# Attention and bilinear FFN on one core: weight sums rescheduled, casts halved, one more plain weight pair, result stores merged and moved ahead of transposing loads

## The chip, the cores and the metric

The kernel runs on 1 core of one Trainium2 chip. The metric is the device time of one launch in microseconds (us), lower is better. A few names: TensorE (PE) does the matmuls, VectorE (DVE) and ScalarE (ACT) the elementwise work, GpSimd (POOL) the casts. The SP queue issues almost all DMA transfers, in program order; the transfers themselves run on the core's 16 DMA engines.

## The reference, cut to what matters

```python
# q, k, v: 8 batches x 8 heads x 576 tokens x 64; attention only inside chunks of 64 tokens
scores = scale * q_c @ k_c.T
attn = exp(scores - max) / sum
x = (attn @ v_c) as 4608 tokens x 512
# then the bilinear FFN, w_a and w_b 512 x 1536, w_out 1536 x 512
out = ((x @ w_a) * (x @ w_b)) @ w_out        # 4608 x 512, float32
```

## The kernel before

The 4608 tokens are 9 blocks of 512, each of two units of 256. Attention prepares the units ahead of the FFN blocks. Units 0 to 5 are transposed on TensorE, the others by transposing loads on the SP queue. In block 0, and for the first `PLAIN` weight pairs of block 1, the two products of the FFN are formed plainly. Everywhere else a Strassen-like scheme (`Group`) uses 28 matmuls instead of 32, and needs sums of weights (`combine_w`) and of tokens (`combine_x`), which VectorE forms.

```python
def combine_w(i):                       # four sums, all at once
    ...
    for o, x0, x1, op in ((t1, b12, b11, SUB), (t3, b22, b12, SUB),
                          (t2, t3, b11, ADD), (t4, b21, t2, SUB)):
        nc.vector.tensor_tensor(out=o, in0=x0, in1=x1, op=op)

def bring(U):                           # a later unit: cast, transposing loads, next loads
    cast(U, "qk"); load(U + 1, "q")
    transpose_dma(U)                    # on the SP queue
    cast(U, "v"); load(U + 1, "kv")

def out_part(K, tg, part):              # a third of one 128-token result tile
    ...
    if part == 2:
        o_sb = o_pool.tile([128, DM], FP32, name="o_sb")        # 3 buffers
        nc.vector.tensor_copy(out=o_sb, in_=out_ps.pop((K, tg)))
        for g in range(2):              # two stores of 64 consecutive rows
            r0 = K * BLK + 256 * u + 128 * g + 64 * c
            nc.sync.dma_start(out=out[r0:r0 + 64, :], in_=o_sb[g * 64:g * 64 + 64, :])

# block 0
for ft in range(NFT):
    ab_step(0, ft)
    if ft % 2:
        combine_w(ft // 2)
    ...
bring(6); bring(7)                      # before block 1 begins (cut: a loop in the source)
```

One result tile holds two chunks of 64 tokens that lie 128 rows apart in `out`. That is why there are two stores per tile.

The softmax here doesn't subtract the row's maximum and nothing guards it: scores larger than these inputs give would overflow.

Of the kernel before, what the change touches and what calls it, by code (L numbers as in the profile page):

```python
# [8 lines left out]


PE_UNITS = 6
PLAIN = 2


@with_exitstack
def kernel(
# [10 lines left out]
    nc = tc.nc  # L27
# [15 lines left out]
    BLK = 512  # L43
# [13 lines left out]
    x_pool = ctx.enter_context(tc.tile_pool(name="xp", bufs=3))  # L57
    s_pool = ctx.enter_context(tc.tile_pool(name="sp", bufs=2))
    ab_pool = ctx.enter_context(tc.tile_pool(name="ab", bufs=2))
    b_pool = ctx.enter_context(tc.tile_pool(name="bsb", bufs=2))  # L60
    c_pool = ctx.enter_context(tc.tile_pool(name="csb", bufs=2))
    o_pool = ctx.enter_context(tc.tile_pool(name="osb", bufs=3))
    psum = ctx.enter_context(tc.tile_pool(name="psum", bufs=4, space=PSUM))
# [14 lines left out]
    def bank(pool=None):  # L78
        if pool is None:
            pool = spread[0]  # L80
            spread.append(spread.pop(0))
        n = {id(psum): "ps", id(psum_b): "pb", id(psum_c): "pc"}[id(pool)]
        return pool.tile([128, 512], FP32, name=n)
# [20 lines left out]
    def cast_ab(i):  # L104
        for n in ("wb", "wa"):
            w_ab[n, i] = wpool.tile([128, NKT, WCOL], FP16, name=f"{n}{i}")
            nc.gpsimd.tensor_copy(out=w_ab[n, i], in_=staged.pop((n, i)))

    w_t = {}

    def combine_w(i):
        wb, wa = w_ab["wb", i], w_ab["wa", i]
        b11, b12, b21, b22 = wb[:, 0:2], wa[:, 0:2], wb[:, 2:4], wa[:, 2:4]
        t1, t2, t3, t4 = [
            wpool.tile([128, 2, WCOL], FP16, name=f"t{j}_{i}") for j in range(1, 5)
        ]
        for o, x0, x1, op in (
            (t1, b12, b11, SUB),
            (t3, b22, b12, SUB),
            (t2, t3, b11, ADD),  # L120
            (t4, b21, t2, SUB),
        ):
            nc.vector.tensor_tensor(out=o, in0=x0, in1=x1, op=op)
        w_t[i] = (t1, t2, t3, t4)

    def load_wo(i):
        staged["wo", i] = st_pool.tile([128, 2, DM], FP32, name="st")
# [4 lines left out]

    def cast_wo(i):
        t = wpool.tile([128, 2, DM], BF16, name=f"wo{i}")
        nc.gpsimd.tensor_copy(out=t, in_=staged.pop(("wo", i)))
        for f in range(2):
            w_out[2 * i + f] = t[:, f, :]


# [48 lines left out]
    def transpose_pe(U, names="qk"):  # L188
        if U not in qkt:
            qkt[U] = qkt_pool.tile([128, 2, 2, NKT, 128], BF16, name="qkt")  # L190
        for n in names:
            w = "qk".index(n)
            src = raw.pop((n, U))
            tp = bank().bitcast(BF16).rearrange("c (i m p) -> c i m p", i=2, m=NKT)
            for i in range(2):
                for m in range(NKT):
                    nc.tensor.transpose(
                        tp[:, i, m, :],
                        src[:, i, 2 * m:2 * m + 2, :].rearrange("p j d -> p (j d)"),
                        identity,  # L200
                    )
            dst = qkt[U][:, w].rearrange("c g m (p i) -> c i m g p", i=2)
            for i in range(2):
                cp = nc.vector.tensor_copy if w == 0 or U == 1 else nc.scalar.copy
                cp(out=dst[:, i], in_=tp[:, i].rearrange("c m (g p) -> c m g p", g=2))
# [98 lines left out]
    def bring(U):  # L304

        cast(U, "qk")
        load(U + 1, "q")
        if U < NU:
            transpose_dma(U)
        cast(U, "v")  # L310
        load(U + 1, "kv")
# [9 lines left out]
    def ab_step(K, ft, c0=0, c1=BLK):  # L321
        xT = x_tiles[K]
        dst = ab_tile(K)
        i, o = divmod(ft * 128, WCOL)
        ps = {}
        for n, pool in (("wb", psum_b), ("wa", psum_c)):
            ps[n] = bank(pool if c1 - c0 == BLK else psum)[:, :c1 - c0]
            for kt in range(NKT):
                nc.tensor.matmul(
                    ps[n],  # L330
                    w_ab[n, i][:, kt, o:o + 128],
                    xT[:, kt, c0:c1],
                    start=(kt == 0),
                    stop=(kt == NKT - 1),
                )
        b_sb = b_pool.tile([128, BLK], FP32, name="b_sb")
        nc.scalar.copy(out=b_sb[:, :c1 - c0], in_=ps["wb"])
        nc.vector.tensor_tensor(
            out=dst[:, ft, c0:c1], in0=ps["wa"], in1=b_sb[:, :c1 - c0], op=MULT
        )  # L340
# [17 lines left out]
    class Group:  # L358
# [22 lines left out]
                        skip_group_check=True,  # L381
                    )

        def staged(self, src, name, pool):
            t = pool.tile([128, 512], FP32, name=name)
            nc.scalar.copy(out=t, in_=src)  # L386
            return t

# [5 lines left out]

        def p6(self):
            self.product(self.B, self.t2, self.s2)
            self.u = self.staged(self.B, "u_sb", c_pool)

        def p2(self):
            self.product(self.A, self.b21, self.x12)  # L400
            self.b = self.staged(self.A, "b_sb", b_pool)

        def p5(self):
            self.product(self.B, self.t1, self.s1)
            self.v = self.staged(self.B, "v_sb", c_pool)

        def p7(self):
            self.C = bank(psum_c)
# [25 lines left out]
    def out_part(K, tg, part):  # L434
        if part == 0:
            out_ps[K, tg] = bank(psum)
        for ft in range(4 * part, 4 * part + 4):
            nc.tensor.matmul(  # L438
                out_ps[K, tg],
                ab_tiles[K][:, ft, tg * 128:tg * 128 + 128],  # L440
                w_out[ft],
                start=(ft == 0),
                stop=(ft == NFT - 1),
            )
        if part == 2:
            u, c = divmod(tg, 2)
            o_sb = o_pool.tile([128, DM], FP32, name="o_sb")
            nc.vector.tensor_copy(out=o_sb, in_=out_ps.pop((K, tg)))  # L448
            for g in range(2):
                r0 = K * BLK + 256 * u + 128 * g + 64 * c  # L450
                nc.sync.dma_start(out=out[r0:r0 + 64, :], in_=o_sb[g * 64:g * 64 + 64, :])

    def out_step(K, tg, parts=1):
        u, c = divmod(tg, 2)
# [23 lines left out]
    with tc.manual_schedule(  # L478
# [51 lines left out]
        load(4)  # L530
        load(5)
        spread[:] = [psum]
        for ft in range(NFT):
            ab_step(0, ft)
            if ft % 2:
                combine_w(ft // 2)
            if ft == 6:
                transpose_pe(2)
            if ft == 7:
                slot(2)  # L540
            if ft == 9:
                slot(None, 2)
# [1 line left out]
        cast(4)  # L544
        cast(5)
        load(6)
        for U in range(PE_UNITS, 8):
            bring(U)

        outs = []  # L550

        def chunk():
            if outs:
                out_part(*outs.pop(0))

        def values_x(U):
            values(U)
            if U % 2:
                combine_x(U // 2)

        for ft in range(2 * PLAIN):
            ab_step(1, ft, 0, 256)
            if ft == 0:
                transpose_pe(3)
            if ft == 2:
                scores(3)
        sums(3)
        inverse(3)
        values_x(3)
        for ft in range(2 * PLAIN):  # L570
            ab_step(1, ft, 256, 512)

        attention = {
            (1, PLAIN, 0): [lambda: transpose_pe(4)],
            (1, PLAIN, 1): [lambda: scores(4)],
            (1, PLAIN + 1, 0): [lambda: sums(4), lambda: inverse(4), lambda: transpose_pe(5)],
            (1, PLAIN + 1, 1): [lambda: scores(5)],
            (1, PLAIN + 2, 0): [lambda: values_x(4)],
            (1, PLAIN + 2, 1): [lambda: sums(5)],
            (1, PLAIN + 3, 0): [lambda: inverse(5)],  # L580
            (1, PLAIN + 3, 1): [lambda: values_x(5), lambda: scores(6)],
            (2, 0, 0): [lambda: sums(6), lambda: inverse(6)],
            (2, 0, 1): [lambda: values_x(6)],
            (2, 1, 0): [lambda: scores(7)],
# [28 lines left out]
        for K in range(1, NBLK):  # L613
            for i in range(PLAIN if K == 1 else 0, NWP):
                if (K, i) in ((1, PLAIN), ) or (K > 1 and i == 1):
                    outs += [(K - 1, tg, p) for tg in range(4) for p in range(3)]
                if K > 1 and i in (0, 3):
                    if K == 2 and i == 0:
                        bring(8)
                    if K + 1 < NBLK:  # L620
                        bring(2 * K + 5 if i == 0 else 2 * K + 6)
                now = Group(K, i)
                now.p1()
                if last:
                    last.add7()
                chunk()
                if last:
                    last.p3()
                attend(K, i, 0)
                now.p6()  # L630
                now.p2()
                if last:
                    last.p4()
                chunk()
                if K == 1:
                    chunk()
                attend(K, i, 1)
                now.p5()
                now.p7()
                last = now  # L640
# [39 lines left out]
```

## Time and profile before

The first measurement gave a median of 331.14 us (3 runs, 330.89 to 333.21).

| what | value | view |
|---|---|---|
| TensorE busy | 303.6 of 330.1 us | the page, part 1 |
| 103 to 320 us: TensorE busy | 216.37 of 217 us, clock 1.00 | windows |
| 18 to 47 us: VectorE busy | 23.91 of 29 us | windows |
| mean of one weight sum (24 of them) | 0.77 us | groups: (5.5 + 4.8 + 4.2 + 4.0) / 24 |
| result stores | 70, 2.4 us to landing | DMA issues |

The table of windows follows: busy time of each engine with instruction counts, then the granted TensorE clock, the mean busy share of the 16 DMA engines (it can pass 1) and GB/s.

```profile
18.00:47.00 29.00, 25.00 (x180) 11.45 (x179) 23.91 (x36) 11.34 (x19) 19.42 (x18) 0.94 1.07 316
94.50:103.00 8.50, 7.96 (x112) 5.29 (x110) 6.04 (x11) 4.95 (x9) 1.04 (x1) 0.81 0.88 197
103.00:320.00 217.00, 216.37 (x2216) 152.11 (x2214) 148.22 (x241) 121.16 (x218) 27.05 (x26) 1.00 0.56 117
```

From 103 us on, TensorE has no idle time to give back. Everything that can be gained lies earlier. Two of TensorE's longer waits in the timeline follow (start, duration, instruction, in brackets the idle time and who ended it). One of 2.80 us for `xT`, from 55.8 us, lies between them and is left out here:

```profile
36.25 0.64 PE L228 MATMUL ps<-qkt 64*64 64x64 bf16 x32 [2.11 <-DVE qkt L205]
...
92.23 0.63 PE L228 MATMUL ps<-qkt 64*64 64x64 bf16 x30 [3.33 <-DVE o_sb L448]
```

The second wait leads to the SP queue. Its timeline shows the first result stores at 87.66 us, behind loads and transposing loads (L210). The `o_sb` of the first store was ready at 68.3 us.

```profile
82.99 1.25 SPq L210 DMA_TRANSPOSE qkt<-k_raw  x1
84.28 1.23 SPq L156 DMA_DIRECT2D st<-in_k_dram  x2
85.55 2.01 SPq L156 DMA_DIRECT2D st<-in_v_dram  x2
87.66 5.64 SPq L451 DMA_DIRECT2D out_dram<-o_sb  x8
```

Later in the same timeline, two q loads behind four stores are issued in 1.32 us together (1.32 to 2.43 us in other such places).

```profile
135.78 6.82 SPq L451 DMA_DIRECT2D out_dram<-o_sb  x4
142.64 1.32 SPq L156 DMA_DIRECT2D st<-in_q_dram  x2
144.08 1.91 SPq L210 DMA_TRANSPOSE qkt<-q_raw  x1
```

### The profile page before, as it was taken

The page shows a single profiled execution, that of the slowest core. Times are in us where ns is not written, and L with a number is a line of the kernel's source. Part 1 is how long each engine was busy: PE and PEld are TensorE (multiplying, and loading weights), DVE is VectorE, ACT ScalarE, POOL GpSimd, SP SyncE. Part 2 cuts the span into 40 slices and gives each one's busy share as a digit, 9 for nine tenths or more (in the row PEclk, how much of TensorE's full clock was granted, in tenths as well). Part 3 has the DMA queues.
Part 4 walks back from the last instruction along what each step waited for, and adds up shares of the span by engine and source line. Part 5 has one row for each costly group of instructions (what it writes and reads, how often), then busy time and mean ns, then how long its engine had stood idle before and what let it go on. Part 6 is the DMA issues. An engine that isn't in the chain of part 4 may idle for free.

```text
span 330.1 us, 7886 instructions
## 1 busy us (share of the span) xinstructions
PE 303.6 (92%) x3222; PEld 205.7 (62%) x3222; DVE 216.7 (66%) x350; ACT 172.2 (52%) x307; POOL 74.6 (23%) x76
## 2 busy tenths in 40 slices
PE   2979784899789999999999999999999999999995
PEld 1534353766556667676777666777776677777743
DVE  3459895746365678587758766857595768666551
ACT  1733355375457655656566566565656464444400
POOL 1566665633213322222121212120000000000000
PEclk9999799999959999999999999999999999999999
DMA  8999999999989999876978596964111111111223
GB/s 238 328 374 284 274 367 230 258 218 246 224 186 236 219 168 233 201 159 162 145 178 179 141 158 163 187 155 110 32 30 38 32 34 34 32 35 43 52 65 96
DMA packets 139331, 53.98 MB, mean 164 GB/s; under 512 B 114592, under 2 KB 133280, under 8 KB 139296
## 3 DMA queue, kind: packets, MB, share of 16 engines
q1 hardware_dynamic: 139136, 53.36, 69.6%
q8 instruction: 25, 0.41, 0.5%
q10 hardware_dynamic: 160, 0.13, 0.2%
q14 instruction: 10, 0.08, 0.1%
HBM read 37.75 MB, written 9.44 MB: 143 GB/s over the span
## 4 chain that ended last, share of the span: by engine, by line
PE 65%; DMA 17%; SPq 8%; DVE 5%; POOL 2%; issue 1%; ACT 1%; ACTq 0%; POOLq 0%; DVEq 0%
PE ps L438 21%; PE pb L375 17%; PE pc L375 11%; PE ps L375 10%; DMA st<-in_moe_w_a_dram 7%; DMA st<-in_q_dram 5%; SPq L156 5%; DMA st<-in_v_dram 4%; PE ps L460 3%; PE ps L243 1%; DVE s L355 1%; SPq L168 1%; SPq L210 1%; PE ps L228 1%; PE ps L276 1%
## 5 line engine op out<-in xcount | busy, mean ns | idle before, releaser
L438 PE MATMUL ps<-wo,ab_sb 128*128 128x512 bf16 x384 | 97.9, 379 | 0.0
L375 PEld LDWEIGHTS <-t 128*128 128x128 f16 x736 | 69.2, 98 | 18.2 <-issue 4.8
L413 DVE TENSOR_TENSOR c_sb<-pc,v_sb 128x512 f32<-128x512 f32 x46 | 31.8, 691 | 55.2 <-ACT v_sb L386 55.2
L375 PE MATMUL pb<-s,t 128*128 128x256 f16 x368 | 56.4, 277 | 0.5 <-ACT u_sb L386 0.5
L375 PE MATMUL ps<-xT,wb 128*128 128x256 f16 x368 | 55.7, 274 | 0.0
L386 ACT COPY u_sb<-pb 128x512 f32<-128x512 f32 x46 | 27.0, 586 | 52.1 <-PE pb L375 52.1
L438 PEld LDWEIGHTS <-ab_sb 128*128 128x128 bf16 x384 | 37.6, 98 | 25.7
L425 DVE TENSOR_TENSOR ab_sb<-pc,c_sb 128x512 bf16<-128x512 f32 x46 | 31.7, 689 | 12.2 <-PE pc L375 11.7
L375 PEld LDWEIGHTS <-wb 128*128 128x128 f16 x368 | 36.3, 99 | 4.5
L425 DVE TENSOR_TENSOR ab_sb<-pb,b_sb 128x512 bf16<-128x512 f32 x46 | 31.5, 685 | 4.4 <-PE pb L375 4.4
L386 ACT COPY v_sb<-pb 128x512 f32<-128x512 f32 x46 | 27.1, 589 | 13.1 <-PE pb L375 12.2
L183 POOL CAST q_raw<-st 128x1024 bf16<-128x1024 f32 x17 | 17.7, 1040 | 71.2 <-DMA st<-in_q_dram 65.6
L414 DVE TENSOR_TENSOR pc<-pc,u_sb 128x512 f32<-128x512 f32 x46 | 31.7, 690 | 0.0
L393 ACT COPY pb<-ps 128x512 f32<-128x512 f32 x46 | 27.3, 594 | 7.7 <-PE ps L375 7.7
L236 ACT ACTIVATE E<-ps 128x512 bf16<-128x512 f32 x34 | 18.6, 594 | 21.8 <-PE ps L228 21.8
L375 PE MATMUL pc<-xT,t 128*128 128x256 f16 x184 | 27.6, 272 | 0.6 <-DVE pc L414 0.5
L375 PE MATMUL pb<-s,wa 128*128 128x256 f16 x184 | 28.1, 276 | 0.0
L375 PE MATMUL pc<-s,t 128*128 128x256 f16 x184 | 28.1, 276 | 0.0
L448 DVE COPY o_sb<-ps 128x512 f32<-128x512 f32 x32 | 21.9, 685 | 9.1 <-PE ps L438 5.0
L183 POOL CAST k_raw<-st 128x1024 bf16<-128x1024 f32 x17 | 17.7, 1040 | 43.8 <-DMA st<-in_k_dram 42.9
L386 ACT COPY b_sb<-ps 128x512 f32<-128x512 f32 x46 | 27.3, 594 | 0.0
L253 ACT ACTIVATE ln<-ps 128x512 f32<-128x512 f32 x34 | 18.6, 595 | 15.6 <-PE ps L243 15.6
(67 smaller groups left out, 312.8 us busy)
## 6 DMA issues: line engine op xcount, KB each, us to landing
out_dram<-o_sb SPq DMA_DIRECT2D x70, 128.0 KB, 2.4
st<-in_v_dram SPq DMA_DIRECT2D x32, 256.0 KB, 4.2
st<-in_q_dram SPq DMA_DIRECT2D x23, 256.0 KB, 4.3
st<-in_k_dram SPq DMA_DIRECT2D x23, 256.0 KB, 3.6
st<-in_moe_w_b_dram SPq DMA_DIRECT2D x6, 512.0 KB, 7.0
st<-in_moe_w_a_dram SPq DMA_DIRECT2D x6, 512.0 KB, 8.0
st<-in_moe_w_out_dram SPq DMA_DIRECT2D x6, 512.0 KB, 7.1
st<-in_q_dram SPq DMA_DIRECT2D x4, 512.0 KB, 5.4
```

Of the source, the lines that this page charges most:

```text
L156: nc.sync.dma_start(out=st[p:p + n, g], in_=src[b, :, s:s + n, :].rearrange("h p d -> p h d"))
L183: eng.tensor_copy(out=raw[n, U], in_=staged.pop((n, U)))
L236: nc.scalar.activation(out=E_of[U][:, j], in_=sc[j], func=AF.Exp, scale=scale)
L253: nc.scalar.activation(out=ln_of[U][:, cl].rearrange("p m n -> p (m n)"), in_=sm[cl], func=AF.Ln)
L375: nc.tensor.matmul(t[:, h * 256:h * 256 + 256], w[:, kt, h * 128:h * 128 + 128], x[:, kt], start=start and h == 0 and kt == 0, stop=h == 1 ...
L386: nc.scalar.copy(out=t, in_=src)
L393: nc.scalar.copy(out=self.B, in_=self.A)
L413: nc.vector.tensor_tensor(out=self.c, in0=self.C, in1=self.v, op=ADD)
L414: nc.vector.tensor_tensor(out=self.C, in0=self.C, in1=self.u, op=ADD)
L425: nc.vector.tensor_tensor(out=self.dst[:, :, c0:c0 + 256], in0=t.rearrange("p (h n) -> p h n", h=2), in1=o.rearrange("p (h n) -> p h n", h=2),
L438: nc.tensor.matmul(out_ps[K, tg], ab_tiles[K][:, ft, tg * 128:tg * 128 + 128], w_out[ft], start=(ft == 0), stop=(ft == NFT - 1),)
L448: nc.vector.tensor_copy(out=o_sb, in_=out_ps.pop((K, tg)))
```

## The change

The intent is to relieve VectorE in block 0 (fewer weight sums there), to shorten its collisions with GpSimd casts (half-size casts), to let more steps be in flight (more buffers), and to get the first stores out earlier and with fewer issues.

```diff
-PLAIN = 2
+PLAIN = 3
 def cast_ab(i):                                   # cast_wo likewise
-            nc.gpsimd.tensor_copy(out=w_ab[n, i], in_=staged.pop((n, i)))
+            for h in (slice(0, 2), slice(2, 4)):
+                nc.gpsimd.tensor_copy(out=w_ab[n, i][:, h], in_=src[:, h])
-    def combine_w(i):
+    def combine_w(i, part):                       # two of the four sums at a time
 ab_step: more PSUM pools for wa, b_sb rotates over four names of c_pool (b_pool dropped)
 out_part:
-            for g in range(2):
-                r0 = K * BLK + 256 * u + 128 * g + 64 * c
-                nc.sync.dma_start(out=out[r0:r0 + 64, :], in_=o_sb[g * 64:g * 64 + 64, :])
+            r0 = K * BLK + 256 * u
+            nc.sync.dma_start(
+                out=out[r0:r0 + 256, :].rearrange("(g c r) d -> c g r d", g=2, c=2)[c],
+                in_=o_sb,
+            )
 block 0:
-            if ft % 2:
-                combine_w(ft // 2)
+            if ft >= 2 * PLAIN + 1:
+                combine_w(*combos.pop(0))         # pairs 3 to 5 (the last two sums in mid block 1), 0 to 2 in block 1's groups
-        for U in range(PE_UNITS, 8):
-            bring(U)
+        bring(6)
+        # bring(7) now inside block 1, in its last group
+        transpose_pe(3)                           # before block 1's steps
 ... (attention of units 3 to 6 shifted accordingly)
```

More of the change, by code (lines that the diff above doesn't have):

```diff
@@ L59 @@
     ab_pool = ctx.enter_context(tc.tile_pool(name="ab", bufs=2))
-    b_pool = ctx.enter_context(tc.tile_pool(name="bsb", bufs=2))
     c_pool = ctx.enter_context(tc.tile_pool(name="csb", bufs=2))
@@ L106, in cast_ab @@
             w_ab[n, i] = wpool.tile([128, NKT, WCOL], FP16, name=f"{n}{i}")
-            nc.gpsimd.tensor_copy(out=w_ab[n, i], in_=staged.pop((n, i)))
+            src = staged.pop((n, i))
+            for h in (slice(0, 2), slice(2, 4)):
+                nc.gpsimd.tensor_copy(out=w_ab[n, i][:, h], in_=src[:, h])
     w_t = {}
-    def combine_w(i):
+    def combine_w(i, part):
         wb, wa = w_ab["wb", i], w_ab["wa", i]
         b11, b12, b21, b22 = wb[:, 0:2], wa[:, 0:2], wb[:, 2:4], wa[:, 2:4]
-        t1, t2, t3, t4 = [
-            wpool.tile([128, 2, WCOL], FP16, name=f"t{j}_{i}") for j in range(1, 5)
-        ]
+        if i not in w_t:
+            w_t[i] = [wpool.tile([128, 2, WCOL], FP16, name=f"t{j}_{i}") for j in range(1, 5)]
+        t1, t2, t3, t4 = w_t[i]
         for o, x0, x1, op in (
-            (t1, b12, b11, SUB),
-            (t3, b22, b12, SUB),
-            (t2, t3, b11, ADD),
-            (t4, b21, t2, SUB),
-        ):
+            ((t1, b12, b11, SUB), (t3, b22, b12, SUB)),
+            ((t2, t3, b11, ADD), (t4, b21, t2, SUB)),
+        )[part]:
             nc.vector.tensor_tensor(out=o, in0=x0, in1=x1, op=op)
-        w_t[i] = (t1, t2, t3, t4)
     def load_wo(i):
@@ L134, in cast_wo @@
         t = wpool.tile([128, 2, DM], BF16, name=f"wo{i}")
-        nc.gpsimd.tensor_copy(out=t, in_=staged.pop(("wo", i)))
+        src = staged.pop(("wo", i))
         for f in range(2):
+            nc.gpsimd.tensor_copy(out=t[:, f], in_=src[:, f])
             w_out[2 * i + f] = t[:, f, :]
@@ L325, in ab_step @@
         ps = {}
-        for n, pool in (("wb", psum_b), ("wa", psum_c)):
-            ps[n] = bank(pool if c1 - c0 == BLK else psum)[:, :c1 - c0]
+        whole = c1 - c0 == BLK
+        for n, pool in (
+            ("wb", psum_b if whole else psum),
+            ("wa", (psum_c, psum)[ft % 2] if whole else psum_c),
+        ):
+            ps[n] = bank(pool)[:, :c1 - c0]
             for kt in range(NKT):
@@ L335, in ab_step @@
                 )
-        b_sb = b_pool.tile([128, BLK], FP32, name="b_sb")
+        b_sb = c_pool.tile([128, BLK], FP32, name=("b_sb", "u_sb", "v_sb", "c_sb")[ft % 4])
         nc.scalar.copy(out=b_sb[:, :c1 - c0], in_=ps["wb"])
@@ L382, in product, with staged @@
                     )
-        def staged(self, src, name, pool):
-            t = pool.tile([128, 512], FP32, name=name)
+        def staged(self, src, name):
+            t = c_pool.tile([128, 512], FP32, name=name)
             nc.scalar.copy(out=t, in_=src)
@@ L396, in p6 @@
             self.product(self.B, self.t2, self.s2)
-            self.u = self.staged(self.B, "u_sb", c_pool)
+            self.u = self.staged(self.B, "u_sb")
         def p2(self):
             self.product(self.A, self.b21, self.x12)
-            self.b = self.staged(self.A, "b_sb", b_pool)
+            self.b = self.staged(self.A, "b_sb")
         def p5(self):
             self.product(self.B, self.t1, self.s1)
-            self.v = self.staged(self.B, "v_sb", c_pool)
+            self.v = self.staged(self.B, "v_sb")
         def p7(self):
@@ L532 @@
         spread[:] = [psum]
+        combos = [(i, p) for i in range(PLAIN, NWP) for p in range(2)]
         for ft in range(NFT):
             ab_step(0, ft)
-            if ft % 2:
-                combine_w(ft // 2)
+            if ft >= 2 * PLAIN + 1:
+                combine_w(*combos.pop(0))
             if ft == 6:
@@ L563 @@
             if ft == 0:
-                transpose_pe(3)
-            if ft == 2:
                 scores(3)
-        sums(3)
-        inverse(3)
-        values_x(3)
+            if ft == 3:
+                sums(3)
+                inverse(3)
+        values(3)
+        while combos:
+            combine_w(*combos.pop(0))
+        combine_x(1)
         for ft in range(2 * PLAIN):
             ab_step(1, ft, 256, 512)
+        combos = [(i, p) for i in range(PLAIN) for p in range(2)]
         attention = {
             (1, PLAIN, 0): [lambda: transpose_pe(4)],
-            (1, PLAIN, 1): [lambda: scores(4)],
-            (1, PLAIN + 1, 0): [lambda: sums(4), lambda: inverse(4), lambda: transpose_pe(5)],
-            (1, PLAIN + 1, 1): [lambda: scores(5)],
-            (1, PLAIN + 2, 0): [lambda: values_x(4)],
-            (1, PLAIN + 2, 1): [lambda: sums(5)],
-            (1, PLAIN + 3, 0): [lambda: inverse(5)],
-            (1, PLAIN + 3, 1): [lambda: values_x(5), lambda: scores(6)],
+            (1, PLAIN, 1): [lambda: scores(4), lambda: transpose_pe(5)],
+            (1, PLAIN + 1, 0): [lambda: sums(4), lambda: inverse(4)],
+            (1, PLAIN + 1, 1): [lambda: values_x(4), lambda: scores(5)],
+            (1, PLAIN + 2, 0): [lambda: sums(5), lambda: inverse(5), lambda: bring(7)],
+            (1, PLAIN + 2, 1): [lambda: values_x(5), lambda: scores(6)],
             (2, 0, 0): [lambda: sums(6), lambda: inverse(6)],
@@ L626 @@
                 chunk()
+                if K == 1:
+                    chunk()
+                    combine_w(*combos.pop(0))
                 if last:
@@ L636 @@
                     chunk()
+                    combine_w(*combos.pop(0))
                 attend(K, i, 1)
```

## The prediction

> **What bounds the kernel now.** The table of windows gives TensorE 216.4 busy of 217.0 us between 103 and 320 us at clock 1.00: that part is TensorE-bound and not touched. Before 18 us the first loads set the pace. The losses lie between 18 and 103 us (TensorE busy 71.0 of 85, partly at half clock). The timeline shows them:
>
> - 34.1 us: 2.1 us idle; scores of unit 2 wait for VectorE's copy of the transposes. Half clock follows (1.5 us lost).
> - 47.0 and 49.4 us: 1.0 and 2.05 us; block 1 waits for VectorE (xT, ab_sb).
> - 55.8 us: 2.8 us; second half of block 1 waits for unit 3's xT.
> - 88.9 us: 3.3 us; PSUM waits for an o_sb copy, itself waiting 4.0 us for its buffer. The SP queue issued the first store at 87.7 us, behind loads and transposing loads of units 6 and 7; its o_sb was ready at 68.3 us. Half clock follows until 97.7 us (2.8 us lost).
> - small ones: about 2.5 us.
>
> Together about 18 us.
>
> **Why VectorE is late.** From 18 to 47 us it is busy 23.9 of 29 us, 15.2 of that in weight sums. One takes 0.41 us, or 1.1 to 1.3 us beside a GpSimd cast (1.04 us each); mean 0.77. This agrees with the Trainium skill, "SBUF — State Buffer", section "Who interferes with whom": a VectorE instruction with two SBUF inputs contends with GpSimd's reads.
>
> **What the change does.**
> - Sums: 10 of 24 in block 0 instead of 20, from column step 7 on; 2 in the middle of block 1, 12 over its three Strassen groups. About 8 us of VectorE time leaves block 0; the 2.1 us stall and its half clock should go.
> - Halved casts bound a collision to about 0.5 us, but q, k, v casts stay whole: small.
> - One more weight pair plain: 32 instead of 28 matmuls of 0.108 us, +0.43 us.
> - More PSUM and b_sb buffers in plain steps: removes waits of 0.2 to 0.3 us.
> - First three stores go ahead of unit 7's transposing loads, one issue each instead of two: the 3.3 us gap and its half clock go.
>
> **What stays or comes.** Value products of unit 2 wait for its v cast (ends 38.9 us): 1 us. Scores of unit 3 queue behind VectorE's backlog: 2.5 us. Second half of block 1: inverse plus xT outlast two steps, 1.5 us, then sums before its multiplies, 1.4 us. In block 1's last groups VectorE needs 8 to 9 us per group against TensorE's 7.7: 1.5 us at the start of block 2. Sum about 8 us.
>
> So 18 - 8 - 0.4 = about 9.5 us, less 1 us for a possible new half-clock stretch (the skill, "TensorE: Matmul & The Clock Gate", section "Why this matters for your kernels", warns of idle gaps over about 3 us; here 2.1 us sufficed once and 2.8 us once did not).
>
> **Predicted: 322.5 us, range 318 to 327.5.** Faster by over 2%: 0.72; within: 0.26; slower: 0.02.
>
> **What would show it.** First store near 78 us; no 3 us TensorE gap near 80 to 90 us, clock 1.00 there; scores of unit 2 without wait; mean weight sum under 0.7 us; block 2's first product near 85 to 87 us instead of 94.5; the rest equally long.
>
> **What would make it wrong.** A longer VectorE backlog between blocks 0 and 1 that drops the clock; sums stalling the Strassen groups; data of units 4 and 5 (casts end 59.1 and 63.9 us) pacing block 1; late transposing loads of units 7 or 8.

## The result and the profile after

The changed kernel takes a median of 362.83 us (4 runs, 361.57 to 365.99), against 331.9 us for the kernel before (4 runs). Its ratio is 1.094 (95% interval 1.085 to 1.103): slower by over 9%, outside the predicted range. Ratios here are the mean time of one kernel's fast runs over that of the other's of the same rounds, so not quite the ratio of the medians quoted. Executions over 1.5% slower than the fastest of the same kernel are left out of the means.

The first 95 us went largely as predicted. The scores of unit 2 no longer wait (their line at 34.58 us has no bracket), the first store is issued at 78.52 us, and the matmul of block 2's second group that is shown below starts at 94.28 us instead of 100.56 us (its first product, at 89.05 us, missed the 85 to 87 us forecast). The first two of these lines are from the changed kernel, the last is from the kernel before:

```profile
34.58 0.45 PE L227 MATMUL ps<-qkt 64*64 64x64 bf16 x32
...
94.28 0.60 PE L378 MATMUL ps<-xT,wb 128*128 128x256 f16 x4
```

```profile
100.56 0.60 PE L375 MATMUL ps<-xT,wb 128*128 128x256 f16 x4
```

The rest did not stay equally long: from there to the end it is 269.9 us instead of 229.5 us. These are the windows of 103 to 300 us, two windows in the first stretch with stores, and two late ones in which only stores run, in the columns explained above:

```profile
82.00:84.00 2.00, 2.00 (x18) 1.42 (x16) 1.36 (x4) 1.64 (x3) 1.04 (x1) 1.00 0.13 45
84.00:86.00 2.00, 1.89 (x41) 0.85 (x40) 0.49 (x1) 1.46 (x3) 0.00 (x0) 1.00 0.13 51
103.00:300.00 197.00, 172.64 (x1788) 118.09 (x1787) 110.38 (x182) 97.32 (x175) 30.18 (x29) 0.94 0.60 130
290.00:292.00 2.00, 2.00 (x49) 1.61 (x47) 1.74 (x4) 0.64 (x2) 0.00 (x0) 1.00 0.13 51
292.00:294.00 2.00, 2.00 (x17) 1.41 (x15) 1.56 (x3) 0.95 (x2) 0.00 (x0) 1.00 0.13 51
```

TensorE is idle for 24 of 197 us, and the clock drops to 0.94. The DMA share stands at 0.13 while stores run. That is 2/16. The waits of TensorE (engine, line, releaser: total us, times, longest):

```profile
PE ps L227 <- DMA qkt<-k_raw: 28.8, 10, 4.8
```

Ten times, TensorE waits for a transposing load. It waited for none before. The SP queue's timeline shows why these loads are late:

```profile
78.52 5.02 SPq L453 DMA_DIRECT2D out_dram<-o_sb  x3
83.59 10.01 SPq L155 DMA_DIRECT2D st<-in_q_dram  x2
93.77 4.09 SPq L209 DMA_TRANSPOSE qkt<-q_raw  x1
97.96 1.25 SPq L209 DMA_TRANSPOSE qkt<-k_raw  x1
...
141.19 1.29 SPq L453 DMA_DIRECT2D out_dram<-o_sb  x2
142.53 8.68 SPq L155 DMA_DIRECT2D st<-in_q_dram  x2
151.33 4.08 SPq L209 DMA_TRANSPOSE qkt<-q_raw  x1
```

The stores are still issued in 0.56 us each (median). Two q loads behind two or three of them take 6.88 to 10.01 us to issue (1.32 to 2.43 us before), and the first transposing load after them mostly about 4 us (1.29 to 2.67 us before, from 93 us on). The view of the critical chain shows the first two q loads one by one:

```profile
83.59 4.96 SPq L155
...
88.61 5.00 SPq L155
```

Each load's issue lasts about as long as one merged store (5.1 us, estimated below). From 84 to 88 us, while the first load is being issued, the DMA share and the rate are those of the stores alone (0.13, 51 GB/s), so that load moves next to nothing yet. The loads do more than share two engines with the stores: they are held up at issue. In blocks with loads, the pairs of stores come 38.4 and 41.1 us apart from block to block (141.19, 179.55, 220.62 us), against 32.1 and 31.6 us in the kernel before (135.78, 167.84, 199.41 us).

The chain that ended last says the same on the page, first before, then after: the SP queue holds 39% of the span (8% before), TensorE only 36% (65% before).

```profile
PE 65%; DMA 17%; SPq 8%; DVE 5%; POOL 2%; issue 1%; ACT 1%; ACTq 0%; POOLq 0%; DVEq 0%
```

```profile
SPq 39%; PE 36%; DMA 13%; DVE 6%; issue 2%; ACT 1%; POOL 1%; POOLq 0%; ACTq 0%; DVEq 0%
```

The Trainium skill, "DMA: Bandwidth & Descriptors", section "Why a DMA increments its semaphore by 16 and not by 1", states how the number of engines of a copy is chosen: the largest number up to 16 that divides the slowest dimension of both access patterns. The merged store's destination is 2x64x512, its source 128x512, so by that rule it gets 2 engines. The store before was 64x512 on both sides, so 16. The share of 0.13 agrees. At 51 GB/s one store of 262,144 bytes then takes about 5.1 us (an estimate from those two numbers).

### The profile page after: what moved, and what is told of

It is laid out like the page before. It is cut to its first block, busy times and chain, and to the rows that moved or that the text cites. A ratio compares the mean times of both kernels' runs of the same rounds, so it can differ in the third digit from the quotient of the medians.

```text
span 364.2 us, 7869 instructions
## 1 busy us (share of the span) xinstructions
PE 311.6 (86%) x3226; PEld 209.4 (58%) x3226; DVE 209.5 (58%) x350; ACT 172.0 (47%) x307; POOL 76.4 (21%) x94
## 4 chain that ended last, share of the span: by engine, by line
SPq 39%; PE 36%; DMA 13%; DVE 6%; issue 2%; ACT 1%; POOL 1%; POOLq 0%; ACTq 0%; DVEq 0%
SPq L155 22%; SPq L209 13%; PE ps L441 10%; PE pb L378 8%; PE pc L378 5%; DMA qkt<-k_raw 5%; PE ps L378 5%; DMA st<-in_v_dram 3%; PE ps L465 2%; DMA st<-in_q_dram 2%; DMA st<-in_moe_w_b_dram 2%; SPq L453 2%; DVE t L122 1%; SPq L167 1%; PE pc L332 1%
## 5 line engine op out<-in xcount | busy, mean ns | idle before, releaser
L441 PE MATMUL ps<-wo,ab_sb 128*128 128x512 bf16 x384 | 101.0, 389 | 0.0
L378 PE MATMUL ps<-xT,wb 128*128 128x256 f16 x360 | 57.2, 284 | 0.0
L441 PEld LDWEIGHTS <-ab_sb 128*128 128x128 bf16 x384 | 38.8, 101 | 28.4 <-issue 3.0
L428 DVE TENSOR_TENSOR ab_sb<-pc,c_sb 128x512 bf16<-128x512 f32 x45 | 30.9, 688 | 17.5 <-PE pc L378 17.2
L227 PE MATMUL ps<-qkt 64*64 64x64 bf16 x544 | 9.0, 203 | 32.5 <-DMA qkt<-k_raw 28.8
L396 ACT COPY pb<-ps 128x512 f32<-128x512 f32 x45 | 26.4, 587 | 12.3 <-PE ps L378 11.4
L227 PEld LDWEIGHTS <-qkt 64*64 64x64 bf16 x576 | 6.9, 115 | 39.6 <-DMA qkt<-k_raw 33.5
L378 PE MATMUL pc<-s,t 128*128 128x256 f16 x180 | 29.4, 290 | 0.0
L378 PE MATMUL pb<-s,wa 128*128 128x256 f16 x180 | 27.3, 275 | 0.1
```

Source lines behind the costliest of these rows:

```text
L378: nc.tensor.matmul(t[:, h * 256:h * 256 + 256], w[:, kt, h * 128:h * 128 + 128], x[:, kt], start=start and h == 0 and kt == 0, stop=h == 1 ...
L396: nc.scalar.copy(out=self.B, in_=self.A)
L428: nc.vector.tensor_tensor(out=self.dst[:, :, c0:c0 + 256], in0=t.rearrange("p (h n) -> p h n", h=2), in1=o.rearrange("p (h n) -> p h n", h=2),
L441: nc.tensor.matmul(out_ps[K, tg], ab_tiles[K][:, ft, tg * 128:tg * 128 + 128], w_out[ft], start=(ft == 0), stop=(ft == NFT - 1),)
```

## The experiments

Theory A: the merged store runs on 2 of 16 DMA engines, and everything that must also pass through those two waits. Rival B: `bring(7)` was moved too late, and the SP queue never catches up. Rival C: one DMA of 256 KB is too large a burst, whatever its shape.

### Stores split again

```diff
-            nc.sync.dma_start(out=out[r0:r0 + 256, :].rearrange(...)[c], in_=o_sb)
+            for g in range(2):
+                r0 = K * BLK + 256 * u + 128 * g + 64 * c
+                nc.sync.dma_start(out=out[r0:r0 + 64, :], in_=o_sb[g * 64:g * 64 + 64, :])
```

> The changed kernel with one thing undone: each 128x512 result tile is stored again by two DMAs of 64 consecutive rows instead of one whose destination is 2x64x512. Theory A (the 2x64x512 store runs on 2 of the 16 DMA engines, and everything queued behind it on those two waits): 323 to 327 us, DMA share never long at 0.13, TensorE without waits for transposing loads after 100 us. Theory B (unit 7's transposing loads issued too late, the queue never catches up): stays at 355 to 365 us.

Measured: 324.39 us, ratio to before 0.973 (0.969 to 0.977). Undoing the merge alone turns 9% slower into nearly 3% faster. From 103 to 300 us TensorE is busy 195.37 of 197 us at clock 1.00, and only one wait for a transposing load is left (1.5 us):

```profile
103.00:300.00 197.00, 195.37 (x2044) 138.47 (x2043) 136.62 (x223) 111.03 (x200) 27.09 (x26) 1.00 0.60 126
```

B is refuted: the order of the queue is that of the changed kernel.

### Merged stores in the kernel before

The diff above, the other way round, on the kernel before.

> The kernel before with only the 2x64x512 store put in. Theory A: clearly slower than before, 350 to 370 us, DMA share near 0.13 after stores, issues of the q loads of about 5 us each on the SP queue. Theory B: 330 to 332 us.

Measured: 368.27 us, ratio 1.104 (1.098 to 1.111). The merged store alone does the harm, without any other part of the change. The late windows show the share of 0.13 and 51 GB/s again, and the two q loads behind the first four stores take 10.64 us to issue, about 5 us each as expected.

### Unit 7's loads early again, merge kept

```diff
-        bring(6)
+        bring(6)
+        bring(7)
-            (1, PLAIN + 2, 0): [lambda: sums(5), lambda: inverse(5), lambda: bring(7)],
+            (1, PLAIN + 2, 0): [lambda: sums(5), lambda: inverse(5)],
```

> The changed kernel with unit 7's loads and transposing loads put back ahead of block 1, merged store kept. Theory A: still 355 to 370 us. Theory B: back to 322 to 326 us.

Measured: 367.95 us, ratio 1.102 (1.094 to 1.109). No recovery, as A expects and B does not. The change of order is not without effect: the waits for transposing loads shrink from 28.8 to 20.9 us, but TensorE now stands once for 9.6 us for an `o_sb` copy.

### One store of 256 KB, but to 128 consecutive rows

The columns of `xT` are written in token order (the multiply writes its 64-column halves 128 columns apart), so a result tile becomes 128 consecutive rows. The result stays correct. The diff is cut: the removed lines and the stores of the last block, which follow the same row order, are left out.

```diff
+            xu = x_tiles[K][:, :, 256 * u:256 * u + 256]
             nc.vector.tensor_tensor(
-                out=x_tiles[K][:, :, c0:c0 + 128],
-                in0=av[cl].rearrange("p m g s -> p m (g s)"),
-                in1=rs[:, cl],
+                out=xu.rearrange("p m (g c s) -> p m g c s", g=2, c=2)[:, :, :, cl],
+                in0=av[cl],
+                in1=rs[:, cl].rearrange("p m (g s) -> p m g s", g=2),
                 op=MULT)
...
+            r0 = K * BLK + 128 * tg
+            nc.sync.dma_start(out=out[r0:r0 + 128, :], in_=o_sb)
```

> The changed kernel with the columns of xT laid out in token order, so that each result tile is 128 consecutive rows: still one DMA of 256 KB per tile, but its destination is 128x512. Result stays correct. Theory A: as fast as the split store, 322 to 327 us. Rival C (one DMA of 256 KB is too large a burst for the queue, whatever its shape): as slow as the changed kernel, 355 to 365 us.

Measured: 323.05 us, ratio 0.968 (0.965 to 0.972). This is the same 256 KB in one DMA, and it costs no time against the split store. C falls. The median landing time of these stores is 2.6 us, and two q loads behind the first three of them are issued in 1.23 us. It beats both kernels; it and the split store have overlapping intervals. Two windows of half a microsecond inside one such store:

```profile
281.00:281.50 0.50, 0.50 (x4) 0.20 (x3) 0.50 (x2) 0.46 (x1) 0.00 (x0) 1.00 0.73 287
281.50:282.00 0.50, 0.50 (x6) 0.40 (x5) 0.43 (x1) 0.00 (x0) 0.00 (x0) 1.00 0.63 238
```

### Four and eight engines

The same single store of 256 KB per tile in the changed kernel, with the destination's outermost size set to 4 or 8. The rows land in a wrong order.

```diff
+            r0 = K * BLK
             nc.sync.dma_start(
-                out=out[r0:r0 + 256, :].rearrange("(g c r) d -> c g r d", g=2, c=2)[c],
+                out=out[r0:r0 + BLK, :].rearrange("(a t b) d -> t a b d", a=4, t=4)[tg],   # or a=8
                 in_=o_sb)
```

> The changed kernel with each tile still stored by one DMA of 256 KB, but its destination split 4x32x512 instead of 2x64x512 (rows land in a wrong order on purpose). If the number of engines is set by the outermost size and their capacity is the limit: four engines, about 0.25 DMA share and 100 GB/s in stretches with stores alone, a store of about 2.6 us instead of 5.1; per block about 19 us of loads plus 10 us of stores on those engines, below TensorE's 32 us, so 324 to 334 us. If any destination of three dimensions is slow, as in 2x64x512: 355 to 365 us.

> As the 4x32x512 run, with 8x16x512 (wrong row order on purpose). By engine count: eight engines, 19 plus 5 us per block, 322 to 327 us, close to the contiguous store. If three dimensions are slow as such: 355 to 365 us.

Measured: 334.93 us with 4 (ratio 1.005, 0.999 to 1.012), 325.48 us with 8 (0.974, 0.968 to 0.981). The run with 4 is a little above its range. Its TensorE waits 8.4 us, five times, for transposing loads; the run with 8 waits 1.0 us, once. The sum behind the range for 4 (about 19 us of loads, an estimate that no view shows directly, plus 10 us of stores, below 32 us) forecasts no such waits, so a sum of busy times alone does not account for this run. Windows inside a store, with 4 and then with 8:

```profile
282.00:283.00 1.00, 1.00 (x11) 0.89 (x10) 0.04 (x1) 0.36 (x1) 0.00 (x0) 1.00 0.25 72
283.00:284.00 1.00, 0.95 (x8) 0.61 (x7) 0.74 (x2) 0.71 (x2) 0.00 (x0) 1.00 0.27 104
288.00:290.00 2.00, 2.00 (x17) 1.42 (x15) 1.70 (x3) 0.58 (x2) 0.00 (x0) 1.00 0.25 92
```

```profile
282.50:283.00 0.50, 0.50 (x7) 0.44 (x6) 0.25 (x1) 0.45 (x1) 0.00 (x0) 1.00 0.43 156
283.00:283.50 0.50, 0.50 (x6) 0.34 (x4) 0.13 (x1) 0.50 (x2) 0.00 (x0) 1.00 0.52 201
```

The shape of three dimensions is not slow in itself. The outermost size of the destination sets the share of the DMA engines, and the rate follows it:

| destination of one 256 KB store | share while it runs | GB/s | time, us |
|---|---|---|---|
| 2x64x512 | 0.13 | 51 | 362.83 |
| 4x32x512 | 0.25 to 0.27 | 72 to 104 | 334.93 |
| 8x16x512 | 0.43 to 0.52 | 156 to 201 | 325.48 |
| 128x512 | 0.63 to 0.73 | 238 to 287 | 323.05 |

### The merged stores issued from the ACT queue

```diff
-            nc.sync.dma_start(
+            nc.scalar.dma_start(
                 out=out[r0:r0 + 256, :].rearrange("(g c r) d -> c g r d", g=2, c=2)[c],
```

> The changed kernel, its 2x64x512 stores issued from the ACT queue instead of the SP queue. If the harm is the order in the SP queue (loads behind stores): 325 to 340 us. If the harm is the capacity of the two DMA engines (about 19 us of loads and 20 us of stores per block, whoever issues them, 39 us against TensorE's 32): still 350 to 370 us, with a block every 37 to 40 us.

Measured: 389.12 us, ratio 1.166 (1.158 to 1.174), above both ranges. The time is no clean test. ScalarE's own work now queues behind stores that are not ready (at 136.00 us it resumes after an idle time of 3.84 us, just after a store was issued at 135.42 us), and TensorE waits for that (first line below). The issue times on the SP queue are of use, though: with none of these stores on that queue, three q loads together still take 8.28 us to issue (2.05 us for three in the kernel before).

```profile
PE pb L378 <- ACT v_sb L389: 35.2, 11, 9.8
```

```profile
125.24 1.93 SPq L155 DMA_DIRECT2D st<-in_v_dram  x2
127.21 8.28 SPq L155 DMA_DIRECT2D st<-in_q_dram  x3
```

So issuing the stores from another queue does not free the loads. This speaks for the two engines, not the SP queue's order alone, as the shared resource. How much of the 40 us is engine capacity and how much is order in the queue stays open.

### What the other parts are worth

Three parts were undone in the contiguous-store kernel, since in the changed kernel the stores hide them. The extra buffers and the third plain pair were never undone alone, so their worth is not shown. First, `bring(7)` early again:

> The contiguous-store kernel (323.1 us, 0.968 of before) with unit 7's loads and transposing loads back ahead of block 1. As predicted for the order of stores: a TensorE wait of about 3 us for an o_sb copy near 85 us returns, with a half-clock stretch, 3 to 6 us longer, 326 to 329 us (0.977 to 0.987 of before). If the order no longer matters once stores are one issue each: 322 to 324 us.

Measured: 331.72 us, ratio 1.001 (0.993 to 1.009), above both ranges. The whole gain is gone. TensorE stands for 7.8 us in the place of the old 3.3 us wait and resumes within 0.5 us of where it did before (92.23 us), because the first stores go out at 87.02 us again:

```profile
91.77 0.64 PE L227 MATMUL ps<-qkt 64*64 64x64 bf16 x30 [7.80 <-DVE o_sb L451]
```

```profile
84.97 1.95 SPq L155 DMA_DIRECT2D st<-in_v_dram  x2
87.02 5.05 SPq L453 DMA_DIRECT2D out_dram<-o_sb  x4
```

All weight sums in block 0 again (the part as in the kernel before, `if ft % 2`, both halves):

> The contiguous-store kernel with all 24 weight sums formed in block 0, as before. As predicted: VectorE late again, the waits for the qkt copy of unit 2 (2 us, perhaps half clock) and at the start of block 1 return, mean weight sum up towards 0.75 us: 3 to 8 us longer, 326 to 331 us. If the extra buffers and the later plain pair are what helped: 322 to 325 us.

Measured: 328.15 us, ratio 0.989 (0.980 to 0.999). The waits return as predicted, the mean weight sum goes back to 0.72 us, and the clock of 47 to 62.6 us falls to 0.84:

```profile
35.82 0.45 PE L227 MATMUL ps<-qkt 64*64 64x64 bf16 x32 [2.01 <-DVE qkt L204]
...
51.35 0.64 PE L227 MATMUL ps<-qkt 64*64 64x64 bf16 x32 [3.23 <-DVE qkt L204]
```

Whole casts of the weights again (one loop pass over `slice(0, 4)` in `cast_ab`, one cast in `cast_wo`):

> The contiguous-store kernel with whole casts of weights (1.04 us each) instead of halves. As predicted a small term: within 1.5 us of 323 us, 0.964 to 0.973 of before.

Measured: 323.09 us, ratio 0.974 (0.965 to 0.984), where the contiguous-store kernel had 323.05 us. The halved casts are worth nothing that these runs can tell. The ratio lies just above the stated one, because the fast runs of the kernel before beside it were themselves shorter (329.66 to 333.81 us) than those beside the contiguous-store kernel (332.34 to 334.52 us). Its time, taken in the same rounds as the two runs above, is a second yardstick for them beside the 323.05 us of the earlier group.

Last, an attempt at a better version (its diff is cut to the second half of block 1): the contiguous-store kernel with value products of unit 2 one step later, scores of unit 3 half a step later, two output chunks of block 0 put into the wait for unit 3's `xT`, and `combine_x(1)` behind the first multiplies of the second half.

```diff
+        outs += [(0, tg, p) for tg in range(4) for p in range(3)]
+        chunk()
+        chunk()
         for ft in range(2 * PLAIN):
             ab_step(1, ft, 256, 512)
+            if ft == 3:
+                combine_x(1)
```

> The contiguous-store kernel with the waits that are left in block 1 attacked: value products of unit 2 one column step later, scores of unit 3 one half step later, two output chunks of block 0 put into the wait for unit 3's xT, token sums of block 1 and the last two weight sums behind the first multiplies of the second half. Expected 2 to 4.5 us shorter: 318.5 to 321 us, 0.955 to 0.963 of before.

Measured: 323.2 us, ratio 0.976 (0.967 to 0.986): a miss, not told apart from the kernel that it was to improve. From 47 to 62.6 us TensorE is busier (14.49 us instead of 11.80), but from 62.6 to 94.5 us it is less busy than in the contiguous-store kernel (26.82 us instead of 29.66), with new waits of 1.2 us each at 63 and 83 us for `o_sb` copies. The waits moved, they did not go.

## Why the prediction was wrong

**The step that failed** is the last under "What the change does": "First three stores go ahead of unit 7's transposing loads, one issue each instead of two". The order was costed, the shape of the store was not. One DMA was booked as two DMAs minus one issue. Its destination of 2x64x512 confines it to 2 engines: 0.13 share, 51 GB/s, about 5.1 us each (the estimate above) where the same bytes on 128 rows land in 2.6 us. With it fell "the rest equally long". Instead of no change after block 2's start, TensorE waits 28.8 us for transposing loads and computes for a while at half clock (busy 311.6 us for the same matmuls that take 300.3 us with contiguous stores). These two, 28.8 and 11.3 us, add up to 40.1 us, where the two profiled spans (364.2 and 321.0 us) are 43.2 us apart.

**What would have shown it beforehand:** the shape of the store's destination, 2x64x512, beside the rule in the skill's DMA page. Both were at hand before the prediction. "Late transposing loads of units 7 or 8" did stand among what could go wrong, without a cause or a cost. Putting unit 7's loads early again did not bring the time back (367.95 us), so their place in the order was not the cause.

**What held.** With the stores spread over all engines, the kernel takes 323.05 us, 0.968 of before, against a predicted 322.5 us of 331.14 us, 0.974. So the rest of the sum was about right, in part by luck, as misses of both signs cancel:

- Sums later: predicted to remove the 2.1 us stall and its half clock. Undone, both return (2.01 us; then a group of four matmuls takes 1.91 us instead of 1.03 us), and a further wait of 3.23 us is followed by half clock too (0.84 in a window): about 5 us in all. (The prediction's "20" counts the sums that ran before 47 us; the code forms all 24 in block 0.)
- Mean weight sum under 0.7 us: 0.58 us in the changed kernel (13.9 us / 24) against 0.77 us before; 10 of the 24 sums took over 1 us before, 2 in the changed kernel. This fits the skill's "SBUF — State Buffer", section "Who interferes with whom".
- Halved casts "small": 323.09 us without them, 323.05 us with them.
- Stores first: booked at 3.3 us and 2.8 us of half clock, measured 8.7 us in medians (331.72 against 323.05). It was undersized, since the late store fixes the time at which TensorE resumes. Whatever the other parts gain before it is then lost in a longer wait.
- What stays: predicted 1, 2.5, 1.5, 1.4 and 1.5 us, about 8 us. Measured in the contiguous-store kernel 1.1, 1.0, 2.3, 1.5 and 2.0 us (0.84, 0.38 and 0.78), so 7.9 us; single terms were off, the sum was not.
- First product of block 2 at 85 to 87 us: 86.39 us with split stores, 89.05 us in the changed kernel, where a wait for an `o_sb` buffer already costs 1.77 us.

**What stays open:** what the issue of the loads waits for on the SP queue (no view shows it; that each takes about the time of one store is a hint, not a proof), and the share of queue order in the loss.

## What to carry to other kernels

Before merging DMAs, look at the outermost size of both sides: here a store with 2 there in its destination ran on 2 engines, and the loads behind it paid. Lay the data out so that the merged transfer keeps a large outermost size; here that was a change of the column order of `xT`, and it cost nothing measurable. A gain ahead of a late store on the same queue was worth nothing here until that store moved (331.72 us), so cost such parts together.

## What the Trainium skill lacked or had wrong

- "DMA: Bandwidth & Descriptors": its rule for the number of engines held (shares of 0.13, 0.25 and about 0.5 for outermost sizes 2, 4 and 8). It lacks what the confined transfer does to others: the issue of two later loads on the SP queue grew from 1.32 to 2.43 us to as much as 10.01 us, about one store's 5.1 us per load (8.28 us for three loads even with the stores on the ACT queue), and the DMA share looks low (0.13) while this happens.
- "TensorE: Matmul & The Clock Gate", section "Why this matters for your kernels", advises against idle gaps over about 3 us. In the kernel before a gap of 2.1 us was followed by half clock, and a gap of 2.8 us was not; in the contiguous-store kernel 2.28 us was not, but in the run with all sums in block 0 the same 2.28 us was (groups of four matmuls took 1.06 us instead of 0.60 us). So in these runs the length of the gap alone does not decide.
- "SBUF — State Buffer": its contention rule agrees with 0.41 us against 1.1 to 1.3 us for the same sum. It does not say whether halving the other engine's instructions pays; here it paid nothing that could be measured (323.09 against 323.05 us).
